# A hand-scheduled attention kernel: new waits and costs in its planner, longer joins on GpSimd, doubled sums

## The chip, the core and the metric

The kernel runs on one core of a Trainium2 chip. Its engines are TensorE (PE, matrix products; PEld in the profile is its weight loads), ScalarE (ACT, exponentials), VectorE (DVE), GpSimd (POOL) and SyncE (SP, which issues most DMAs). The metric is the device time of one execution in microseconds (us), median over runs.

## The reference

Two independent attention blocks of 32 heads with 16 columns each, on 2048 rows of 512, side by side in the output. Block A is linear attention, block B full softmax attention:

```python
# A
phi = lambda t: jnp.where(t > 0, t + 1, jnp.exp(t)) + 1e-6
pq, pk = phi(q), phi(k)
kv = jnp.einsum("bhsd,bhse->bhde", pk, v)
z = jnp.einsum("bhsd->bhd", pk)
o = jnp.einsum("bhqd,bhde->bhqe", pq, kv) / (jnp.einsum("bhqd,bhd->bhq", pq, z)[..., None] + 1e-6)
# B
scores = jnp.einsum("bhqd,bhkd->bhqk", q, k) * scale
o = jnp.einsum("bhqk,bhkd->bhqd", softmax(scores), v)
# both: q, k, v = x @ wqkv before, @ wo behind
```

B's scores are 32 x 2048 x 2048 numbers, and nearly all the time goes into their exponentials.

## The kernel before

**Blocks.** B's scores are made in blocks of 128 keys by 512 queries for one head. Four groups of eight heads, four stretches of 512 queries and two halves (even and odd heads) give 32 units; a unit has 4 heads (`g`, one in each quarter of TensorE's rows) times 16 blocks of keys, 64 blocks. A block's scores are one product QT,KM (L871, `qk`) into a bank of PSUM.

**Two ways to the exponential.** Either ScalarE applies Exp to two or three neighbouring banks of the tile pS at once and writes float16 to PT (L1084, in `fill_act_cand`). There are two such slots (`SCR`); a spare bank between them makes a slot three banks wide. Or VectorE does it without an exponential: it multiplies a block's scores (in pD or the spare bank) by a constant, adds another and stores int16 (L987, `p1`); the bits, read as float16, are a rough exponential. To smooth its error the block is used three times: the pattern itself, and two copies of it with a constant added to the bits, `SHIFT = (328, 656)`. Two blocks make a group of 1024 columns in one of eight buffers of DI (`DG`, `NDG`). The copies are made by GpSimd (L1176, `on_pool`) or, the second one alone and when GpSimd's queue is long, by VectorE (L1141, `on_dve`). GpSimd can make two copies of two groups in one instruction: two equal patterns, or the first of one group and the second of another, which it then makes out of that group's first (`mixed`).

**Sums.** The products with the values (L1253, `pv_cand`) add up numerator and denominator of four heads in one bank pPV: a block of PT takes one product with VV; a pattern takes one with VX (the values times `VW`, which weights the uncopied pattern, made by GpSimd in `v4_job`) and one with VV for each copy. A unit's sums go through VectorE (L1282, L1287, `unit_done`), GpSimd (L1288) and VectorE.

**The rest** are jobs in between: B's projections (L600, L677; K is spread to KM by DMAs on SP's queue), all of A (L718 to L783, with its own exponentials L693), and the output products (L809) and stores on SP's queue. PAR's column of SBUF is an operand of VectorE's L614, which makes the first K blocks.

**The order.** Every engine runs a fixed order of instructions, which a planner in the kernel's Python code writes when the program is built. It simulates the five lanes (`T`, with a clock for each), offers candidates (an exponential's two or three score products, `fill_act_cand`; more pattern blocks, `fill_d_cand`; products with the values, `pv_cand`; jobs, `job_cand`; what waits in `cands`), and takes the earliest, with priorities. It counts a duration for each instruction and a wait between engines: `LAT = 0.12` in most places, `LPE` behind a given engine. `SEG` is a table of 26 settings that change each 12 us of the planner's clock (limits on backlogs, how much earlier TensorE may run, when a second copy goes to VectorE, a seed for ties). `fill_in` puts products without a use into TensorE's gaps. On the chip semaphores keep the order safe, so a wrong duration costs waits and no correctness.

Of the kernel before, what the change touches and what calls it, by code (L numbers as in the profile page):

```python
# [238 lines left out]
def bass_concat_heads__linear_attn_block__softmax_full_mha__prompt_kernel(nc, A_x, A_wqkv, A_wo, B_x, B_wqkv, B_wo, out):  # L239
# [18 lines left out]
    VW = 1.5546875  # L258
    SHIFT = (328, 656)
    PMX = 0.0  # L260
# [64 lines left out]
    )  # L325
    GB = 0.0
    PM = -0.1
# [32 lines left out]
    with es:  # L360
# [51 lines left out]
        FLG = sb("FLG", [1, 1], F32)  # L412

# [75 lines left out]
        sch.add("dve", lambda e: e.memset(ZW[:], 0.0), writes=["ZW"])  # L489
        mk_ident(identb, "identb")  # L490
# [34 lines left out]
        LAT = 0.12  # L525
        LPE = {"dve": 0.04, "act": 0.19, "pool": 0.0, "pe": 0.12, "dma": 0.12}
# [6 lines left out]
        class Shared(float):  # L533

            pass

# [8 lines left out]
        class Job:  # L545
# [11 lines left out]
            def stage_done(self, i, end, bk, bi):  # L557
                if i == self.rel and bi is not None:
                    dfree[bi] = end + LPE[self.stages[i][0]]
                    held[bi] = False  # L560
                for st, tk in self.gives:
                    if st == i:
                        tok[tk] = end + LAT
                if i + 1 < len(self.stages):
                    eng, dur, fn = self.stages[i + 1]
                    lat = LAT if eng != "pe" or eng != self.stages[i][0] else 0.0
                    push(eng, end + lat, self.prio if eng == "pe" else (0 if eng == "act" or i + 1 <= self.rel and self.bank else min(self.prio, 2)), dur,
                         lambda st_, en_, fn=fn: (fn(bk), self.stage_done(i + 1, en_, bk, bi)))
# [10 lines left out]
        MM = 0.26  # L579
# [50 lines left out]
        def gram_x(t4, **kw):  # L630
# [6 lines left out]
            return Job(halves(mm, [("xTb", t) for t in ts], n=16, parts=2, dur=0.07) +  # L637
# [3 lines left out]
        def gram_w(kind, **kw):  # L641
# [5 lines left out]
            return Job(halves(mm, [("Wb", kind, g) for g in range(NGP)], n=16, parts=2, dur=0.07) +  # L647
# [8 lines left out]
        def flag_job(**kw):  # L656
            def f(e, bk):
# [6 lines left out]
                ("pe", 0.5, f_pe(f, [("TOP", i) for i in range(3)] + ["identf"])),  # L664
# [7 lines left out]
        def v4_job(t4, Gp, **kw):  # L672
# [7 lines left out]
            st = halves(mm, [("Wb", 2)] + [("xTb", t) for t in ts], n=16, parts=2, dur=0.07)  # L680
# [3 lines left out]
            st.append(("pool", 0.7, f_op("pool", lambda e: e.tensor_scalar(  # L684
# [29 lines left out]
        def akv_mm(t2, hp, kind):  # L714
# [5 lines left out]
            return chunked(halves(mm, ["WaK", ("xA", b)], n=8, parts=2, dur=0.14), 4 * hp + t2 // 4)  # L720
# [19 lines left out]
        def akvsum_job(hp, bl, **kw):  # L740
# [3 lines left out]
            st = halves(mm, [("KNa", t) for t in range(NT)] + [("VNa", t) for t in range(NT)] + ["VNa1"], n=16, parts=4, dur=0.085)  # L744
# [17 lines left out]
        def aden_job(sc, **kw):  # L762
# [6 lines left out]
            return Job(halves(mm, [("PQT", 0, bq) for bq in range(4)] + [("RHA", bq) for bq in range(4)] + [("RHZ", bq) for bq in range(4)], n=16, parts=2, dur=0.04) +  # L769
# [4 lines left out]
        def anum_job(sc, tl, **kw):  # L774
# [7 lines left out]
            return Job([("pe", 0.36, f_pe(f, [("PQT", 0, bq) for bq in range(4)] + [("RHA", bq) for bq in range(4)])),  # L782
# [143 lines left out]
        def d_pick(at, used, bi=None):  # L926
# [11 lines left out]
            if not dgroup["open"]:  # L938
                buf = min((i for i in range(NDG) if dgfree[i] is not None), key=lambda i: dgfree[i], default=None)
# [29 lines left out]
        def d_emit(tk, en):  # L969
# [4 lines left out]
            for b, buf, bi in tk:  # L974
# [23 lines left out]
                waiting[bi] = (buf, b, push("dve", en + LAT, 0, 0.6, p1))  # L998
# [17 lines left out]
        def fill_act_cand():  # L1016
# [16 lines left out]
            start = max(T["pe"], t0, afree[sl] + LAT, pw[0] - 0.5)  # L1033
            dur = 0.33 if pmode[0] != "q" else 0.23
            if nfill[0] >= 2 and not (u == NU - 1 and left[u] < DEND) and not lagging(start):
                lim = T["act"] + sum(exps) - dur - LAT - RW
# [4 lines left out]
            def run(st, en):  # L1041
# [25 lines left out]
                if len(bl) + len(tk) > 4:  # L1067
                    en += 0.21
# [418 lines left out]
        def fill_in(st):  # L1487
# [4 lines left out]
            if n <= 0:  # L1492
                return
# [188 lines left out]
```

## Time and profile before

| | |
|---|---|
| median of 2 runs | 661.1 us (661.04 to 661.15) |
| the profiled execution | 660.98 us, of which the profile's span is 659.2 us |
| TensorE's granted clock over the span | 0.999 |
| instructions | PE 6609, DVE 1089, ACT 686, POOL 450 |

A row of the groups reads: line, engine, operation, out<-in with shapes, count, then busy us, mean ns of one, and behind the last bar the engine's idle time before them with what ended it. A row of the timeline or of the chain begins with the start in us and the duration; xN merges N instructions. A row of the windows has the busy us of PE, PEld, DVE, ACT and POOL in this order, and in parentheses the instructions. A row of the waits has the us in total, the times and the longest. Records of neighbouring instructions overlap on an engine, so what one costs in a full queue is the spacing of starts, not the record's length.

### The profile page before, as it was taken

The numbers are of one execution on the slowest core, as the hardware profiler recorded it, in microseconds if no ns is written. First come the engines' busy times: TensorE is split into PE (matmuls) and PEld (weight loads), VectorE is DVE, ScalarE is ACT, GpSimd is POOL, SyncE is SP. The second block draws the span as 40 slices with busy tenths as digits, with TensorE's granted clock in tenths as the row PEclk, the third lists the DMA queues.
The fourth block names the chain that finished last, engine by engine and source line by source line (L and its number), as shares of the span: only waits on it lengthen the run. The fifth ranks groups of instructions, "written<-read, shape, count | busy, mean of one in ns | idle before, by whom it ended". The sixth has DMA issues, their size and how long they took to land.

```text
span 659.2 us, 15950 instructions
## 1 busy us (share of the span) xinstructions
PE 633.3 (96%) x6609; PEld 200.4 (30%) x6662; DVE 632.1 (96%) x1089; ACT 644.7 (98%) x686; POOL 592.7 (90%) x450
## 2 busy tenths in 40 slices
PE   8999999999999999999999999999999999999997
PEld 6323333222333333332222233322222223232222
DVE  4999999999999999999999999999999999999995
ACT  6999999999999999999999999999999999999994
POOL 5999999999999999999998899999999999999983
PEclk9999999999999999999999999999999999999999
DMA  9701010020102101210012011010011000120102
GB/s 178 207 3 33 1 34 6 11 43 9 34 2 33 21 14 33 65 34 9 9 27 64 17 34 34 18 19 10 7 26 41 17 1 11 25 26 25 33 26 67
DMA packets 53213, 21.53 MB, mean 33 GB/s; under 512 B 44177, under 2 KB 52625, under 8 KB 53137
## 3 DMA queue, kind: packets, MB, share of 16 engines
q1 hardware_dynamic: 51664, 19.80, 13.9%
q8 instruction: 54, 0.88, 0.6%
q10 hardware_dynamic: 1472, 0.66, 0.4%
q14 instruction: 23, 0.18, 0.1%
HBM read 4.46 MB, written 4.19 MB: 13 GB/s over the span
## 4 chain that ended last, share of the span: by engine, by line
ACT 96%; PE 3%; DMA 1%; ACTq 0%; issue 0%; DVE 0%; DVEq 0%
ACT PT L1084 93%; ACT EA L693 2%; DMA Wb<-in_B_wqkv_dram 1%; PE pPV L1253 1%; PE pD L809 1%; PE pS L871 0%; PE pD L1305 0%; PE pS L1305 0%; PE pS L1389 0%; ACTq L442 0%; PE pD L1389 0%; DVE KNa L582 0%; PE pD L659 0%; PE pD L871 0%; DVEq L1626 0%
## 5 line engine op out<-in xcount | busy, mean ns | idle before, releaser
L1084 ACT ACTIVATE PT<-pS 128x1024 f16<-128x1024 f32 (+1 forms) x648 | 636.6, 1305 | 1.0 <-PE pS L871 1.0
L1176 POOL TENSOR_SCALAR DI<-DI 128x2048 int16<-128x2048 int16 (+1 forms) x369 | 554.4, 1503 | 47.3 <-DVE DI L987 20.2
L987 DVE TENSOR_SCALAR DI<-pD 128x512 int16<-128x512 f32 x492 | 324.4, 679 | 6.1 <-PE pD L871 2.5
L871 PE MATMUL pS<-QT,KM 32*128 32x512 bf16 x1556 | 255.0, 384 | 8.8 <-ACT PT L1084 4.5
L1253 PE MATMUL pPV<-PT,VV 128*17 128x512 f16 x1369 | 233.7, 381 | 0.0
L1253 PE MATMUL pPV<-DI,VV 128*17 128x512 f16 x1358 | 227.3, 382 | 0.0
L871 PE MATMUL pD<-QT,KM 32*128 32x512 bf16 x492 | 170.5, 384 | 0.3 <-DVE PQT L696 0.3
L1253 PE MATMUL pPV<-DI,VX 128*17 128x512 f16 x679 | 161.0, 381 | 0.2 <-DVE OT L1282 0.2
L871 PEld LDWEIGHTS pS<-QT,KM 32*128 32x128 bf16 x1556 | 64.6, 91 | 265.3 <-ACT PT L1084 227.4
L987 DVE TENSOR_SCALAR DI<-pS 128x512 int16<-128x512 f32 x187 | 126.6, 677 | 0.7
L1141 DVE TENSOR_SCALAR DI<-DI 128x1056 int16<-128x1056 int16 x113 | 77.0, 687 | 0.5
L1253 PEld LDWEIGHTS pPV<-PT,VV 128*17 128x17 bf16 x1369 | 47.5, 88 | 41.4 <-issue 36.1
L1253 PEld LDWEIGHTS pPV<-DI,VV 128*17 128x17 bf16 x1358 | 47.0, 88 | 40.4 <-issue 33.0
L871 PEld LDWEIGHTS pD<-QT,KM 32*128 32x128 bf16 x492 | 40.5, 91 | 5.4 <-DVE DI L987 2.0
L1253 PEld LDWEIGHTS pPV<-DI,VX 128*17 128x17 bf16 x679 | 34.2, 88 | 22.0 <-issue 17.7
L718 PE MATMUL pD<-Wa,xTa 128*128 128x256 bf16 x200 | 30.5, 275 | 0.3 <-DVE DI L987 0.2
L600 PE MATMUL pD<-xTb,Wb 128*128 128x512 bf16 x67 | 21.2, 383 | 3.1 <-issue 2.3
L1282 DVE STREAM_TRANSPOSE OT<-pPV 128x512 f32<-128x512 f32 x31 | 21.9, 705 | 0.1
L582 DVE CAST KNa<-pD 128x512 bf16<-128x512 f32 x27 | 18.4, 681 | 3.0 <-PE pD L809 2.0
L1288 POOL TENSOR_TENSOR OT<-OT,ZR 128x256 bf16<-128x256 f32 x31 | 19.3, 621 | 1.6
L718 PEld LDWEIGHTS pD<-Wa,xTa 128*128 128x128 bf16 x200 | 15.4, 97 | 13.3 <-issue 6.3
L693 ACT ACTIVATE EA<-pD 128x512 bf16<-128x512 f32 x23 | 19.2, 835 | 0.0
(136 smaller groups left out, 346.3 us busy)
## 6 DMA issues: line engine op xcount, KB each, us to landing
out_dram<-KNa SPq DMA_DIRECT2D x31, 128.0 KB, 1.7
Wa<-in_A_wqkv_dram SPq DMA_DIRECT2D x1, 1536.0 KB, 8.2
KM<-KR SPq DMA_DIRECT2D x96, 16.0 KB, 1.8
Wb<-in_B_wqkv_dram SPq DMA_DIRECT2D x2, 384.0 KB, 4.5
Wb<-in_B_wqkv_dram SPq DMA_DIRECT2D x1, 512.0 KB, 4.6
Wa<-in_A_wo_dram SPq DMA_DIRECT2D x1, 512.0 KB, 4.5
Wa<-in_B_wo_dram SPq DMA_DIRECT2D x1, 512.0 KB, 3.7
ON<-in_B_x_dram ACTq DMA_DIRECT2D x1, 256.0 KB, 3.1
```

The source lines that it names most:

```text
L582: return lambda e, bk: (e.tensor_copy(out_fn(), in_fn(bk)) if lane == "dve" else e.activation(out_fn(), in_fn(bk), ACTF.Copy))
L600: return e.matmul(f32v(bk), lhsT=Wb[:, cc, kind * 512 + Gp * 128:kind * 512 + Gp * 128 + 128], rhs=xTb[:, cc, sc * 512:(sc + 1) * 512], st ...
L693: ("act", 0.052 + n * 0.000833, f_ev("act", lambda e, bk: e.activation(EA[:, 0:n], f32v(bk)[:, c0:c0 + n], ACTF.Exp), [], ["EA"])),
L718: return e.matmul(f32v(bk)[:, 256 * tt:256 * tt + 256], lhsT=xTa[:, b, cc, (o + tt) * 128:(o + tt + 1) * 128], rhs=Wa[:, cc, 512 * kind + ...
L871: return e.matmul(dst, lhsT=KM[32 * g:32 * g + 32, Gp % 2, e_, j * 128:(j + 1) * 128], rhs=QT[32 * g:32 * g + 32, Gp % 2, c * 512:(c + 1) ...
L987: sch.add("dve", lambda e: e.tensor_scalar(DI[:, di_at(0, buf) + i * 512:di_at(0, buf) + (i + n) * 512], f32v(DBANK[b0], n * 512), ESC, EB ...
L1084: sch.add("act", lambda e: e.activation(PTf[:, p0 * 512:p0 * 512 + w], S5[:, c0:c0 + w], ACTF.Exp, scale=SC), reads=skeys(sl, len(bl)), wr ...
L1141: sch.add("dve", lambda e: e.tensor_scalar(gapped(DI, di_at(v, buf), wide // 32, 32), DI[:, di_at(0, buf) - 32:di_at(0, buf) + w], 1.0, fl ...
L1176: sch.add("pool", lambda e: e.tensor_scalar(dv, sv, 1.0, sh_, op0=ALU.mult, op1=ALU.add), reads=keys, writes=[("DI", v_, x) for x, v_ in s ...
L1253: sch.add("pe", lambda e, g=g, j=j, c0=c0, V_=V_, r2=r2, P=P, first=first, last_=last_: e.matmul(PVb[32 * g:32 * g + 17, 0:512] if len(P.s ...
L1282: sch.add("dve", lambda e: e.transpose(OT[:, 0, :], PVb[:, 0:512]), reads=[("PV", g) for g in range(4)], writes=[("OT", 0)])
L1288: ("pool", 0.7, f_op("pool", lambda e: e.tensor_tensor(xn[:, :, 16 * e_:16 * e_ + 16], o[:, :, 0:16], zr.unsqueeze(2).broadcast_to([128, 1 ...
```

## The change

1. **The planner's waits.** `LAT` goes. A wait is looked up by the pair of engines (`LTO`) or by the engine that ends (`LPE`), and a change of kind among TensorE's products (scores, values, jobs) costs `SWT` in `pe_at`. Durations of jobs become shorter (a product of 512 columns 0.216 instead of 0.26). A score slot counts as free 0.426 after its exponential ends, where it was 0.07 + 0.12.
2. **The choice.** A product may come ahead of an exponential's scores only if it ends before `lim + KSL`. Products without a use go only into gaps of `FIDLE` = 0.8 or more. Pattern buffers are taken in turn.
3. **GpSimd's joins.** Up to `JN` = 4 copies of the same pattern from buffers at equal steps go into one instruction; the mixed pairs go. The planner counts `PFX` = 0.157 an instruction, where it counted 0.276.
4. **Doubled sums.** The constants that the copies add grow by 1024, which doubles the float16 value, `VW` doubles, and ScalarE's exponential gets a bias of ln 2 out of a column of SBUF, so that all terms of a sum double and the quotient stays.
5. **The table** `SEG` is new from end to end, so that the order on all engines changes.

```diff
-    VW = 1.5546875
-    SHIFT = (328, 656)
-    PMX = 0.0
+    VW = 2 * 1.5546875
+    SHIFT = (1352, 1680)
...
-    PM = -0.1
+    PM = 0.09
+    JN = 4
+    KSL = 0.02
+    PFX = 0.157
+    FIDLE = 0.8
...
+        LN2 = sb("LN2", [128, 1], F32)
+        sch.add("dve", lambda e: e.memset(LN2[:], 0.6931471805599453), writes=["LN2"])
...
-        LAT = 0.12
-        LPE = {"dve": 0.04, "act": 0.19, "pool": 0.0, "pe": 0.12, "dma": 0.12}
+        LPE = {"dve": 0.136, "act": 0.426, "pool": PM, "pe": 0.2, "dma": 0.12}
+        LTO = {("pe", "dve"): 0.2, ("pe", "act"): 0.215, ("act", "dve"): 0.4, ("dve", "pool"): 0.163, ("pool", "dve"): 0.07, ("dve", "act"): 0.15}
+        SWT = 0.106
+        def pe_at(md):
+            return T["pe"] + (0.0 if pmode[0] in (md, None) else SWT)
...
-                buf = min((i for i in range(NDG) if dgfree[i] is not None), key=lambda i: dgfree[i], default=None)
+                buf = min((i for i in range(NDG) if dgfree[i] is not None), key=lambda i: (dgfree[i] > at, (i - dgroup["buf"] - 1) % NDG), default=None)
...
-            start = max(T["pe"], t0, afree[sl] + LAT, pw[0] - 0.5)
-            dur = 0.33 if pmode[0] != "q" else 0.23
+            start = max(pe_at("q"), t0, afree[sl], pw[0] - 0.43)
+            dur = 0.214
...
-                    sch.add("act", lambda e: e.activation(PTf[:, p0 * 512:p0 * 512 + w], S5[:, c0:c0 + w], ACTF.Exp, scale=SC),
-                            reads=skeys(sl, len(bl)), writes=[("PT", p0 + i) for i in range(len(bl))])
-                    afree[sl] = en_ + 0.07
+                    sch.add("act", lambda e: e.activation(PTf[:, p0 * 512:p0 * 512 + w], S5[:, c0:c0 + w], ACTF.Exp, bias=LN2[:, 0:1], scale=SC),
+                            reads=skeys(sl, len(bl)) + ["LN2"], writes=[("PT", p0 + i) for i in range(len(bl))])
+                    afree[sl] = en_ + LPE["act"]
...
                 def on_pool(st_, en_):
-                    d1 = lambda b_: dgroup["st"][b_].get("v1", 1e9)
-                    two = [x for x in pshift if x[2] == w and x[1] != buf and x[3][0] <= st_ + PMW
-                           and (x[0] == v or d1(x[1] if v == 1 else buf) <= st_ + PMX)]
...
-                        T["pool"] = en_ = st_ + 0.276 + 2 * w * 0.00083
-                    mixed = len({v_ for _, v_ in segs}) == 2
+                    near_ = {x[1]: x for x in pshift if x[0] == v and x[2] == w and x[3][0] <= st_ + PMW}
+                    best = [buf]
+                    for step in range(1, NDG):
+                        run_ = [buf]
+                        while len(run_) < JN and run_[-1] + step in near_:
+                            run_.append(run_[-1] + step)
+                        while len(run_) < JN and run_[0] - step in near_:
+                            run_.insert(0, run_[0] - step)
+                        if len(run_) > len(best):
+                            best = run_
...
+                    T["pool"] = en_ = st_ + PFX + len(best) * w * 0.000834
+                    moves = [(di_at(0, b_), di_at(v, b_)) for b_ in best]
...
-                        return bass.AP(one.tensor, one.offset, [list(one.ap[0]), [offs[1] - offs[0], 2], [1, w]])
+                        return bass.AP(one.tensor, one.offset, [list(one.ap[0]), [offs[1] - offs[0], len(offs)], [1, w]])
...
-                    me = [(v, buf, w, push("pool", t_ + LAT + 0.05, 0, 0.276 + w * 0.00083, on_pool), rk)]
+                    me = [(v, buf, w, push("pool", t_ + LTO["dve", "pool"], 0, PFX + w * 0.000834, on_pool), rk)]
...
-            if n <= 0:
+            if n <= 0 or st - T["pe"] < FIDLE:
                 return
...
-                lim = max(dry - fa[1] - LAT - 0.05, fa[0])
-                keep = [o for o in opts if o[2] != "pe" or o[4] is fa[2] or o[0] + o[3] <= lim or o[0] + 1e-9 < fa[0] - o[3]]
+                lim = max(dry - 0.43, fa[0])
+                swt = lambda o: 0.0 if fd is not None and o[4] is fd[2] else SWT
+                keep = [o for o in opts if o[2] != "pe" or o[4] is fa[2] or o[0] + o[3] + swt(o) <= lim + KSL]
```

More of the change, by code (lines that the diff above doesn't have):

```diff
@@ L646, in gram_w @@
             gw = GRW[:, kind, :].rearrange("p (a h) -> p a h", h=8)
-            return Job(halves(mm, [("Wb", kind, g) for g in range(NGP)], n=16, parts=2, dur=0.07) +
+            return Job(halves(mm, [("Wb", kind, g) for g in range(NGP)], n=16, parts=2, dur=0.0555) +
                        [("dve", 0.6, f_ev("dve", lambda e, bk: e.tensor_reduce(GRW[:, kind, :], f32v(bk).rearrange("p (h c) -> p h c", c=16), axis=AX.X,
@@ L663, in flag_job @@
                                                 reads=[("GRX", i) for i in range(4)], writes=[("TOP", 0)])),
-                ("pe", 0.5, f_pe(f, [("TOP", i) for i in range(3)] + ["identf"])),
+                ("pe", 0.4, f_pe(f, [("TOP", i) for i in range(3)] + ["identf"])),
                 ("dve", 0.45, f_ev("dve", lambda e, bk: e.tensor_reduce(TP1[:, 0:3], bk[0][0:1, bk[2]:bk[2] + 384].rearrange("p (a n) -> p a n", n=128),
@@ L781, in f @@
                 return ins
-            return Job([("pe", 0.36, f_pe(f, [("PQT", 0, bq) for bq in range(4)] + [("RHA", bq) for bq in range(4)])),
+            return Job([("pe", 0.22, f_pe(f, [("PQT", 0, bq) for bq in range(4)] + [("RHA", bq) for bq in range(4)])),
                         ("dve", 0.6, f_ev("dve", lambda e, bk: e.tensor_tensor(
@@ L997, in p1 @@
                     chain(buf)
-                waiting[bi] = (buf, b, push("dve", en + LAT, 0, 0.6, p1))
+                waiting[bi] = (buf, b, push("dve", en + 0.2, 0, 0.598, p1))
         dgroup["st"] = {}
@@ L1066, in run @@
                     tk.append(d_take(pk))
-                if len(bl) + len(tk) > 4:
-                    en += 0.21
+                en = st + 0.214 * max(sum(x[2] == g for x in bl + [y[0] for y in tk]) for g in range(4))
+                T["pe"] = en
+                en = st + 0.214 * max(sum(x[2] == g for x in bl) for g in range(4))
                 c0 = 0 if sl == 0 else 1024 if ax else 1536
@@ L1110, in run @@
                     tk.append(d_take(pk2))
+                    if tk[0][0][2] == tk[1][0][2]:
+                        T["pe"] = en = en + 0.214
                 d_emit(tk, en)
-            return at, 0.32 if pmode[0] != "q" else 0.22, run
+            return at, 0.214, run
         def close_group():
@@ L1166, in on_pool @@
-                    mixed = len({v_ for _, v_ in segs}) == 2
-                    moves = sorted((di_at(1 if mixed and v_ == 2 else 0, b_), di_at(v_, b_)) for b_, v_ in segs)
+                    near_ = {x[1]: x for x in pshift if x[0] == v and x[2] == w and x[3][0] <= st_ + PMW}
[8 more added lines that the diff above has]
+                            best = run_
@@ new lines, in on_pool @@
+                    keys = []
+                    for b_ in best:
+                        x = near_.get(b_, me[0])
+                        pshift.remove(x)
+                        if b_ != buf:
+                            cands["pool"].remove(x[3])
+                            st_ = max(st_, x[3][0])
+                        keys += [("DI", 0, b_, i) for i in range(n)]
+                    T["pool"] = en_ = st_ + PFX + len(best) * w * 0.000834
+                    moves = [(di_at(0, b_), di_at(v, b_)) for b_ in best]
@@ L1242, in pv_cand @@
             bt = bb[2]
[L1243 removed]
+            dur = 0.218 * bb[1]
             def run(st, en):
@@ L1359, in fin @@
                                               reads=kst(tl), queue="act" if tl == 2 else "sp", force_signal=True))
-                    urgent2.append(Job([("pe", 0.22, last), (lane, 0.6 if lane == "dve" else 0.52, fin)], [("onh", h), ("tail", tl)], [], bank=False))
+                    urgent2.append(Job([("pe", 0.216, last), (lane, 0.6 if lane == "dve" else 0.52, fin)], [("onh", h), ("tail", tl)], [], bank=False))
         def warm(n):
@@ L1462, in job_cand @@
             best = None
-            bi = min((i for i in range(NB + JX) if dfree[i] is not None), key=lambda i: (max(dfree[i], T["pe"]), i), default=None)
+            bi = min((i for i in range(NB + JX) if dfree[i] is not None), key=lambda i: (max(dfree[i], pe_at("j")), i), default=None)
             for lst, pr in ((urgent, 0.5), (early, 2), (bjobs, 2.2), (urgent2, 2.3), (ajobs, AJP)):
@@ L1502, in fill_in @@
                 dst, wr, acc = DB[0:17, db[0] * 512:db[0] * 512 + 256], ("D", db[0]), None
-            elif any(a_ is not None and a_ + LAT <= T["pe"] and i != tail["so"] for i, a_ in enumerate(afree)):
-                sl = min(i for i in range(2) if afree[i] is not None and afree[i] + LAT <= T["pe"] and i != tail["so"])
+            elif any(a_ is not None and a_ <= T["pe"] and i != tail["so"] for i, a_ in enumerate(afree)):
+                sl = min(i for i in range(2) if afree[i] is not None and afree[i] <= T["pe"] and i != tail["so"])
                 g, first = 0, True
```

85 lines of the change are left out of this document (31 added, 54 removed), and 102 rows, old and new, of the table SEG.

## The prediction

> **What bounds the kernel now.** I read the page first, for the busy shares and the chain that ended last.
>
> ```profile
> span 659.2 us, 15950 instructions
> PE 633.3 (96%) x6609; PEld 200.4 (30%) x6662; DVE 632.1 (96%) x1089; ACT 644.7 (98%) x686; POOL 592.7 (90%) x450
> ...
> ACT 96%; PE 3%; DMA 1%; ACTq 0%; issue 0%; DVE 0%; DVEq 0%
> ```
>
> Four engines are 90% busy or more, but the chain is ScalarE's for 96% of the span. The view by windows, asked for the steady part from 60 to 600 us, says how hard:
>
> ```profile
> 60.00:600.00 540.00, 523.26 (x5525) 162.22 (x5565) 531.45 (x911) 540.00 (x580) 499.55 (x354) 1.00 0.12 24
> ```
>
> The fourth busy number is ScalarE's: 540.00 of 540.00. The timeline and the chain of waits give its two ends:
>
> ```profile
> 8.73 37.01 ACT PT L1084 x37
> ...
> 291.69 9.17 ACT PT L1084 x10
> ```
> ```profile
> 629.01 20.77 ACT L1084 ACTIVATE PT<-pS 128x1024 f16<-128x1024 f32 x18
> ```
>
> The exponentials run from 8.73 us to 629.01 + 20.77 = 649.8 us; ahead stand 8.7 us of loads and first projections, behind 9.4 us of last products and stores. The span of 659.2 plus 1.8 outside it is the profiled execution's own 660.98 us, 0.1 below the median of 661.1. So the time moves only if the stretch of 641 us does: by fewer blocks for ScalarE, or by another price for each. The price is 9.17 / 10 = 0.917 us from one exponential of two blocks to the next, or 0.46 us a block.
>
> The groups by shape say how the 2048 blocks (4 groups of heads, 8 units, 64 blocks each) are divided:
>
> ```profile
> L1084 ACT ACTIVATE PT<-pS 128x1024 f16<-128x1024 f32 x575 | 560.5, 1260 | 0.0
> L1084 ACT ACTIVATE PT<-pS 128x1536 f16<-128x1536 f32 x73 | 121.5, 1664 | 1.0 <-PE pS L871 1.0
> ```
> ```profile
> L987 DVE TENSOR_SCALAR DI<-pD 128x512 int16<-128x512 f32 x492 | 324.4, 679 | 6.1 <-PE pD L871 2.5 <-PE pS L871 1.2
> L987 DVE TENSOR_SCALAR DI<-pS 128x512 int16<-128x512 f32 x187 | 126.6, 677 | 0.7
> L1141 DVE TENSOR_SCALAR DI<-DI 128x1056 int16<-128x1056 int16 x113 | 77.0, 687 | 0.5
> ```
> ```profile
> L1176 POOL TENSOR_SCALAR DI<-DI 128x2048 int16<-128x2048 int16 x198 | 376.3, 1900 | 28.1 <-DVE DI L987 13.9 <-POOL DI L1176 2.0 <-DVE RD L770 0.2
> L1176 POOL TENSOR_SCALAR DI<-DI 128x1024 int16<-128x1024 int16 x169 | 176.9, 1047 | 18.2 <-DVE DI L987 6.3
> ```
>
> ScalarE takes 575 x 2 + 73 x 3 = 1369 blocks in 648 instructions. VectorE turns 492 + 187 = 679 into int16 patterns. Each pair of these (a group) needs two shifted copies of 1024 elements; 113 copies are VectorE's and about 198 x 2 + 169 = 565 GpSimd's, in 367 instructions (1.54 copies each). A block leaves ScalarE only if VectorE and GpSimd have time for it.
>
> **The change, part by part.**
>
> *Joins of up to four.* Two doubles that follow each other, and two singles:
>
> ```profile
> 249.99 3.88 POOL L1176 TENSOR_SCALAR DI<-DI 128x2048 int16<-128x2048 int16 x2 [0.40 <-DVE DI L987]
> ...
> 301.27 2.17 POOL L1176 TENSOR_SCALAR DI<-DI 128x1024 int16<-128x1024 int16 x2
> ```
>
> From start to start a double takes 3.88 - 1.90 = 1.98 us and a single 2.17 - 1.05 = 1.12. A copy's elements cost 1.90 - 1.05 = 0.85, so 0.27 is the price of an instruction. Joins save only that. The new rule joins only equal patterns in evenly spaced buffers, so the old pairs of first and second pattern are lost; and a queue that often runs dry cannot offer four copies:
>
> ```profile
> POOL DI L1176 <- DVE DI L987: 15.9, 42, 1.0
> POOL DI L1176 <- POOL DI L1176: 1.9, 12, 0.2
> ```
>
> (GpSimd's waits from 60 to 600 us.) The ends are no gain in joins, 1.54, and four everywhere, 565 / 4 = 141 instructions. I take 2.2, 257 instructions, between the row of doubles, which is nearest, and what a longer queue adds. It saves (367 - 257) x 0.27 = 30 us of GpSimd.
>
> What is that worth? Move x blocks off ScalarE and y copies from VectorE back to GpSimd; all three must fall by the same 0.46x. VectorE's prices stand in its timeline:
>
> ```profile
> 17.50 0.68 DVE L987 TENSOR_SCALAR DI<-pS 128x512 int16<-128x512 f32 x1
> 18.10 0.68 DVE L987 TENSOR_SCALAR DI<-pD 128x512 int16<-128x512 f32 x1
> 18.70 0.74 DVE L614 TENSOR_SCALAR KM<-pD,PAR 128x512 bf16<-128x512 f32 x1
> 19.35 0.69 DVE L1141 TENSOR_SCALAR DI<-DI 128x1056 int16<-128x1056 int16 x1
> 19.96 0.74 DVE L614 TENSOR_SCALAR KM<-pD,PAR 128x512 bf16<-128x512 f32 x1
> 20.62 0.68 DVE L681 CAST VV<-pD 128x512 bf16<-128x512 f32 x1
> ```
>
> An eviction is 18.10 - 17.50 = 0.60, a shifted copy 19.96 - 19.35 = 0.61. VectorE: 0.60x - 0.61y = -0.46x, so y = 1.74x. GpSimd: (0.85 + 0.27 / 2.2)(x + y) - 30 = -0.46x, or 3.12x = 30, x = 9.6. ScalarE falls by 9.6 x 0.46 = 4.4 us. The ends are 0 without joins and, with 61 us saved at a copy price of 0.92, x = 20.5 and 9.4 us.
>
> *Exponentials with a bias.* Sums double: the copies go up by 1024 more (an octave of the bit pattern), VW doubles, and all 640-odd exponentials take `bias=LN2[:, 0:1]`, a column in SBUF, where no bias was given. No row shows ScalarE with such an operand. VectorE's nearest does: with PAR's column an eviction of that size takes 19.35 - 18.70 = 0.65 and 20.62 - 19.96 = 0.66 against 0.60, so 0.06 us more. The ends are 0 and 0.06 an instruction; a fetch can only add, which excludes a gain. I take 0, because the engines overlap differently: VectorE's records exceed their spacing by 0.68 - 0.60 = 0.08, and by 0.74 - 0.655 = 0.08 with the column, so nothing hid there; ScalarE's exceed it by 1.26 - 0.917 = 0.34, so an exponential is under way 0.34 us before its predecessor is done, more than a fetch of 0.06. ScalarE is the chain, so if that cover fails it all shows: 643 x 0.06 = 39 us.
> The Trainium skill (ScalarE: Activation LUTs, What ACT_TABLE_LOAD costs) speaks against this part: it gives 186 ns plus 0.833 ns an element with immediate operands, about 93 ns more for each pointer operand, and an overlap of 93 ns between neighbours. No run here shows that price; by it the sum would be an estimated 643 x 0.093 = 60 us longer, 716 us.
>
> *LN2's memset* is one small VectorE instruction before the first exponential, where VectorE waits anyway; its wait on ScalarE is met before 8.73 us. Nothing:
>
> ```profile
> 0.00:8.70 8.70, 7.24 (x71) 6.38 (x71) 2.82 (x12) 2.47 (x4) 7.45 (x26) 1.00 0.83 164
> ```
>
> VectorE (third) is busy 2.82 of 8.70 us. Without that cover it costs about 0.1.
>
> *Waits in the planner, SWT, the rule with KSL.* These add no instruction; they move instructions in the five fixed orders. The old planner took a score buffer as free 0.07 + 0.12 = 0.19 us after an exponential; the waits say:
>
> ```profile
> PEld pS L871 <- ACT PT L1084: 227.4, 522, 0.7
> ```
>
> 227.4 / 522 = 0.44 a time, and behind that wait TensorE's weight products queue. The new 0.426 puts other products ahead of it. But ScalarE has no idle time between 60 and 600 us to recover, so the gain is 0. At worst a product put ahead overruns; the start of the next exponential is late next. From the other side, what better waits can free is VectorE's 540 - 531.45 = 8.5 us and GpSimd's 15.9 + 1.9: half of both is x = (8.9 + 1.6 x 4.3) / 3.12 = 5, or 2.3 us (1.6 is GpSimd's 0.97 a copy by VectorE's 0.61).
>
> *FIDLE* drops filler products in gaps under 0.8 us. There are 24, none of use to the result, and with TensorE 523 of 540 us busy the clock (the 1.00 in the row) has no reason to fall: nothing. *The new order and the round robin of buffers* move the K spreads and stores on SP's queue, each behind the same producer as before, and no transfer stands in the steady chain; the product of VX stays one GpSimd instruction a tile. Nothing on the sum, 1 us either way for the tail.
>
> **The sum.** Start 8.7 as before, exponentials 641.1 - 4.4 + 0, tail 9.4 as before, 1.8 outside the span: 656.6 us against 661.0, or 656.7 on the scale of the median. Its own range is 649 (four everywhere, and half the waits) to 661 (no gain).
>
> **The rivals.**
>
> *The column costs on ScalarE (slower).* For it: VectorE pays in full for PAR's. Against it: the 0.34 us of overlap. With VectorE's 0.06 it is 656.7 + 39 = 695 us; the engines differ, so I spread the price from half to one and a half of that, 0.03 to 0.09, which gives 676 to 715 us. It decides from 0.03 upward, since 643 x 0.028 = 18 us takes the time past 2%. The order stays fixed, so nothing moves to the engines that then idle. The page of the Trainium skill named above speaks for this case.
>
> *GpSimd is planned too cheap.* The new formula has 0.157 an instruction where the trace has 0.27. On 257 instructions the plan lacks 257 x 0.113 = 29 us. GpSimd's spare time in the steady part is 15.9 + 1.9 of 540, 21 us over the stretch. If the plan fills it as full as now, 8 us are left over; products wait for copies, TensorE's queue stands, and exponentials start late: 656.7 + 8 = 665 us, still within 2%. For it: every such pair in the timeline shows 0.27. Against it: VectorE and not GpSimd may be filled first. It decides once 21 us are used up.
>
> *More than the sum.* Four everywhere and all the waits recovered: 661.1 - 9.4 - 4.6 = 647 us. Against it is the dry queue.
>
> *The change doesn't do what it says:* joins stay at 1.54, 661 us; this is the end of my range.
>
> **How the numbers follow.** The sum's case, 649 to 661, has 0.37; GpSimd too cheap, 661 to 673, 0.21; the column, 676 to 715, 0.34, which is high because the one row with a column shows its price in full; more than the sum, 0.08. A measurement of this kernel can tell about 2% from no change, 648 to 674. So faster is 0.08, same 0.37 + 0.21 = 0.58, slower 0.34. The range must reach into the column's case: 648 to 704 leaves out 0.08 below and, with prices spread evenly, 11 / 39 of 0.34 = 0.10 above.
>
> **What would show it.** Joins: fewer L1176 rows, with shapes of 3072 or 4096 elements, about 257 in all, and fewer shifted copies of VectorE. Blocks: about 1359 instead of 1369 products of PT. Column: the spacing of exponentials in the chain, 0.917 (free) or 0.98 to 1.01. GpSimd too cheap: TensorE or ScalarE waiting on GpSimd, and idle time in ScalarE's 60 to 600 us. The prediction is wrong if that spacing grows by more than 0.03 us, or if ScalarE falls under 99% there.

## The result and the profile after

The changed kernel takes 731.58 us (median of 2 runs, 730.18 and 732.98) against 661.1: 1.107 times as long, 95% interval 1.098 to 1.116. I had forecast 656.7 in a range of 648 to 704. The measured time lies outside it: 70 us were lost where 4 were to be won.

The page of the profile after (the profiled execution took 732.98 us), first the busy shares, then the chain that ended last:

```profile
span 731.2 us, 15899 instructions
...
PE 655.8 (90%) x6646; PEld 202.2 (28%) x6646; DVE 636.1 (87%) x1074; ACT 699.5 (96%) x682; POOL 615.0 (84%) x457
...
ACT 93%; PE 3%; DMA 1%; SPq 1%; DVE 0%; issue 0%; DVEq 0%
```

The span grew by 72.0 us and ScalarE's busy time by 54.8, with four instructions fewer on it. ScalarE is still the chain. Two pieces of the exponentials in the chain of waits, ten of them in a row and a long piece near the end:

```profile
271.15 10.04 ACT PT L1099 x10
...
657.81 57.33 ACT PT L1099 x49
```

Ten take 10.04 us, where the ten at 291.69 took 9.17 before: 0.087 us more each. (Over all of them, the commonest spacing of starts goes from 0.904 to 0.995 us for two blocks and from 1.331 to 1.422 for three, 0.091 more in both.) The view by windows, the steady part:

```profile
60.00:600.00 540.00, 488.45 (x5016) 147.69 (x5013) 487.65 (x818) 527.35 (x520) 471.05 (x319) 1.00 0.09 20
```

ScalarE, the fourth number, has 12.65 us without work where it had none, though each instruction of it takes longer. The timeline of ScalarE shows where most of that is, in two stretches without work (holes, below), and TensorE's beside it shows what stood in front (the number in brackets is the idle time before the row, and what ended it):

```profile
512.48 13.48 ACT L1099 ACTIVATE PT<-pS,LN 128x1024 f16<-128x1024 f32 x13
535.43 11.16 ACT L1099 ACTIVATE PT<-pS,LN 128x1024 f16<-128x1024 f32 x11 [9.47 <-PE pD L887]
549.37 2.12 ACT L1099 ACTIVATE PT<-pS,LN 128x1024 f16<-128x1024 f32 x2 [2.78 <-PE pD L887]
```
```profile
528.67 1.89 PE L616 MATMUL pD<-xTb,Wb 128*128 128x512 bf16 x8
530.40 1.03 PE L616 MATMUL pS<-xTb,Wb 128*128 128x512 bf16 x4
531.26 1.03 PE L616 MATMUL pD<-xTb,Wb 128*128 128x512 bf16 x4
533.55 0.38 PE L887 MATMUL pD<-QT,KM 32*128 32x512 bf16 x1 [1.26 <-DVE KR L635]
```

From 525 us on the last group's projections of K and Q come in a burst, and from 524.4 to 533.5 us no score product runs. The chain of waits shows what they wait for. K is cast into one of two buffers of KR and spread from there to KM by eight DMAs, so the third cast can't start before the first one's spread has landed, and until then its projection holds the bank pD that a score product needs. SyncE's queue, the chain and VectorE:

```profile
526.55 4.96 SPq L640 DMA_DIRECT2D KM<-KR  x8
```
```profile
530.93 1.79 DMA KM<-KR
```
```profile
532.80 0.69 DVE L635 CAST KR<-pD 128x512 bf16<-128x512 f32 x1 [2.26 <-DMA KM<-KR]
```

In the kernel before the last four casts of K start within 44 us, from 442 to 486; here within 8, from 526 to 534.

The groups by shape:

```profile
L1099 ACT ACTIVATE PT<-pS,LN 128x1024 f16<-128x1024 f32 x567 | 612.7, 1440 | 12.6 <-PE pD L887 12.3 <-PE pS L887 0.4
L1191 POOL TENSOR_SCALAR DI<-DI 128x2048 int16<-128x2048 int16 x182 | 345.3, 1897 | 27.4 <-DVE DI L1003 15.6
...
L1191 POOL TENSOR_SCALAR DI<-DI 128x1024 int16<-128x1024 int16 x173 | 180.7, 1044 | 35.9 <-DVE DI L1003 23.8
...
L1099 ACT ACTIVATE PT<-pS,LN 128x1536 f16<-128x1536 f32 x77 | 143.1, 1859 | 1.0 <-PE pS L887 1.0
```

ScalarE has 567 x 2 + 77 x 3 = 1365 blocks (1369 before). GpSimd has 173 single copies, 182 doubles, 16 triples and one of four: 589 copies in 372 instructions, 1.58 each where there were 1.54 (four small ones of 512 are left out). The joins of up to four hardly came about.

For a tally I call ScalarE's lost time what passes between the start of its first exponential and the end of the last beyond the usual spacings (0.904 or 0.995 us for two blocks, 1.331 or 1.422 for three, 0.477 for A's exponentials): 19.6 us, where it was 8.8. Of the 19.6, 12.6 are idle time. So 644 x 0.091 = 58.6 us is the exponentials' price, 10.8 the lost time, 4.2 the tail (13.6 us from the last exponential on, 9.4 before), 0.3 the start, and -1.8 the four blocks: 72.1 for 72.0. That is a tally and no cause yet, since the order of all engines changed with the price.

### The profile page after: what moved, and what is told of

Same layout as the page of the kernel before. It is cut to its first block, busy times and chain, and to the rows that moved or that the text cites. A ratio compares the mean times of both kernels' runs of the same rounds, so it can differ in the third digit from the quotient of the medians.

```text
span 731.2 us, 15899 instructions
## 1 busy us (share of the span) xinstructions
PE 655.8 (90%) x6646; PEld 202.2 (28%) x6646; DVE 636.1 (87%) x1074; ACT 699.5 (96%) x682; POOL 615.0 (84%) x457
## 4 chain that ended last, share of the span: by engine, by line
ACT 93%; PE 3%; DMA 1%; SPq 1%; DVE 0%; issue 0%; DVEq 0%
ACT PT L1099 91%; ACT EA L709 2%; PE pPV L1266 1%; DMA xTb<-in_B_x_dram 1%; PE pS L887 1%; PE pD L825 1%; SPq L640 1%; DMA KM<-KR 0%; DMA out_dram<-KNa 0%; PE pS L825 0%; PE pS L1402 0%; DVE KR L635 0%; DVE KNa L598 0%; PE pS L1318 0%; PE pD L616 0%
## 5 line engine op out<-in xcount | busy, mean ns | idle before, releaser
L1099 ACT ACTIVATE PT<-pS,LN 128x1024 f16<-128x1024 f32 (+1 forms) x644 | 694.1, 1490 | 13.7 <-PE pD L887 12.3
L1191 POOL TENSOR_SCALAR DI<-DI 128x1024 int16<-128x1024 int16 (+2 forms) x376 | 576.1, 1532 | 83.4 <-DVE DI L1003 58.5
L1003 DVE TENSOR_SCALAR DI<-pD 128x512 int16<-128x512 f32 x492 | 328.9, 682 | 39.1 <-PE pD L887 22.7
L1266 PE MATMUL pPV<-DI,VV 128*17 128x512 f16 x1366 | 232.3, 383 | 0.0
L1266 PE MATMUL pPV<-DI,VX 128*17 128x512 f16 x683 | 155.0, 383 | 0.1
L1003 DVE TENSOR_SCALAR DI<-pS 128x512 int16<-128x512 f32 x191 | 130.1, 681 | 6.5 <-PE pS L887 4.6
L1158 DVE TENSOR_SCALAR DI<-DI 128x1056 int16<-128x1056 int16 x89 | 60.3, 685 | 0.2
L734 PE MATMUL pD<-Wa,xTa 128*128 128x256 bf16 x200 | 29.8, 275 | 0.0
L616 PE MATMUL pD<-xTb,Wb 128*128 128x512 bf16 x96 | 26.6, 382 | 0.0
L709 ACT ACTIVATE EA<-pD 128x512 bf16<-128x512 f32 x26 | 24.3, 934 | 0.0
L1301 POOL TENSOR_TENSOR OT<-OT,ZR 128x256 bf16<-128x256 f32 x31 | 19.2, 620 | 4.0 <-DVE ZR L1300 1.9
```

Of the source, the lines that this page charges most:

```text
L616: return e.matmul(f32v(bk), lhsT=Wb[:, cc, kind * 512 + Gp * 128:kind * 512 + Gp * 128 + 128], rhs=xTb[:, cc, sc * 512:(sc + 1) * 512], st ...
L709: ("act", 0.052 + n * 0.000833, f_ev("act", lambda e, bk: e.activation(EA[:, 0:n], f32v(bk)[:, c0:c0 + n], ACTF.Exp), [], ["EA"])),
L734: return e.matmul(f32v(bk)[:, 256 * tt:256 * tt + 256], lhsT=xTa[:, b, cc, (o + tt) * 128:(o + tt + 1) * 128], rhs=Wa[:, cc, 512 * kind + ...
L1003: sch.add("dve", lambda e: e.tensor_scalar(DI[:, di_at(0, buf) + i * 512:di_at(0, buf) + (i + n) * 512], f32v(DBANK[b0], n * 512), ESC, EB ...
L1099: sch.add("act", lambda e: e.activation(PTf[:, p0 * 512:p0 * 512 + w], S5[:, c0:c0 + w], ACTF.Exp, bias=LN2[:, 0:1], scale=SC), reads=skey ...
L1158: sch.add("dve", lambda e: e.tensor_scalar(gapped(DI, di_at(v, buf), wide // 32, 32), DI[:, di_at(0, buf) - 32:di_at(0, buf) + w], 1.0, fl ...
```

## The experiments

All times are medians beside runs of the kernel before on the same chip (660.94 to 661.18 us). An "order" is the order in which the planner writes the instructions. Where an edit shows a piece of a line, the rest of the line stays.

| kernel | us | ratio to before, 95% |
|---|---|---|
| column alone, order before (e2) | 717.85 | 1.084 to 1.088 |
| after without the column (e1) | 701.75 | 1.060 to 1.064 |
| after without column and doubling (e3) | 698.28 | 1.054 to 1.058 |
| e3 with only the constants doubled (e7) | 701.9 | 1.059 to 1.064 |
| e3, GpSimd at 0.273 (e4) | 684.21 | 1.033 to 1.037 |
| e3, table searched anew (e12) | 687.07 | 1.038 to 1.041 |
| e4, table searched anew (e10) | 666.48 | 1.007 to 1.010 |
| e10 with column and doubling (e13) | 723.31 | 1.092 to 1.096 |
| after, GpSimd at 0.273 (e11) | 741.73 | 1.120 to 1.124 |
| before, GpSimd at 0.157 (e6) | 696.75 | 1.052 to 1.056 |
| before, GpSimd at 0.290 (e9) | 687.58 | 1.039 to 1.043 |
| e4 without SWT (e5) | 702.56 | 1.059 to 1.064 |
| e3 without SWT (e8) | 700.84 | 1.058 to 1.062 |

### The column

**e1: ln 2 as an immediate.** The values stay doubled.

```diff
-ACTF.Exp, bias=LN2[:, 0:1], scale=SC)
+ACTF.Exp, bias=0.6931471805599453, scale=SC)
```

> The changed kernel with the bias of ln 2 as an immediate number of the instruction and no column; nothing else moves, the order of every engine is the same. Theory A (the column costs on every exponential, 644 x 0.091 us = 59 us, and the rest of the 70 us is the order's: 10 us more waiting of ScalarE in the stretch and 4.5 us more tail): the spacing of doubles falls from 0.995 back to 0.904 us, time 673 us. Theory B (column alone, the order's holes come from ScalarE being slower than planned and go with it): 657 to 661 us. Theory C (the new order as a whole costs, an immediate other than zero costs as much as a column): stays near 730 us.

Measured: 701.75 us, between the theories; none was whole. The chain of waits has the old price again (8.26 / 9 = 0.918), and the view by windows shows ScalarE with 28.7 us of idle time:

```profile
492.38 8.26 ACT PT L1099 x9
```
```profile
60.00:600.00 540.00, 508.77 (x5212) 162.69 (x5234) 496.97 (x853) 511.30 (x542) 492.06 (x335) 1.00 0.10 21
```

The waits from 60 to 600 us name what is new in it:

```profile
PEld pPV L1266 <- POOL DI L1191: 27.2, 54, 1.4
...
PE pPV L1266 <- POOL DI L1191: 8.7, 19, 0.9
```

In the same instructions with the column, the first of these waits was this:

```profile
PEld pPV L1266 <- POOL DI L1191: 2.2, 9, 0.3
```

So the column had slowed ScalarE until GpSimd was no longer late. ScalarE's lost time is 19.6 us with the column and 48.4 without: 28.8 us appear as 58.6 go, and of the medians 731.58 - 701.75 = 29.8 us are left as the column's cost in this order.

**e2: a column of zeros in the kernel before** (the column ZC and its memset are added). Order and values are those of before.

```diff
-ACTF.Exp, scale=SC)
+ACTF.Exp, bias=ZC[:, 0:1], scale=SC)
```

> The kernel before with one thing added: its exponentials read their bias of 0 out of a column of zeros in SBUF. Order, copies and sums are those of before. Theory A: 648 x 0.091 us = 59 us more, 720 us. If a column cost what it costs VectorE, 0.06: 700 us. If the column cost only in the new order: 661 us.

Measured: 717.85 us, 56.9 more. ScalarE is busy for all of the 540 us again, and does less in them (534 instructions for 580):

```profile
60.00:600.00 540.00, 491.14 (x5065) 146.49 (x5096) 499.17 (x838) 540.00 (x534) 457.68 (x329) 1.00 0.11 22
```

In an order that keeps ScalarE full, every exponential pays: 56.9 / 648 = 0.088 us, measured on the whole.

### The price of a GpSimd instruction in the planner

**e3: no doubling either.** e1 with the old constants, the old VW and no bias: the change's planner, joins and table alone.

```diff
-    VW = 2 * 1.5546875
-    SHIFT = (1352, 1680)
+    VW = 1.5546875
+    SHIFT = (328, 656)
```

> The changed kernel with the sums as before: copies by +328 and +656, the single weight, no bias; its planner, joins, table and order stay. All theories: the same as with the immediate bias within 1 us, since only data differ. If the doubled values themselves mattered to an engine, the two differ.

Measured: 698.28 us. The new order alone costs 37 us, and TensorE's waits on GpSimd stay (24.4 us of weight loads from 60 to 600).

**e4: the traced price.** e3 with one number:

```diff
-    PFX = 0.157
+    PFX = 0.273
```

> As the run without doubling, but the planner counts 0.273 us an instruction for GpSimd's copies, as the trace has it, in place of 0.157. The order changes with it and its table was not made for it, so a few us either way are the order's luck. If GpSimd planned too cheap cost time (rival of the prediction), TensorE's waits on GpSimd go and the time falls below that run's; if GpSimd is not what is waited for, it is the same or slower, 673 to 685 us.

Measured: 684.21 us, 14.1 less. The waits on GpSimd are gone (0.7 us of weight loads), and ScalarE's idle time from 60 to 600 us falls from 27.9 to 10.7. The loss that is left, 23 us, is something else: 8.8 us of it are a longer tail (18.2 us).

**e6: the mirror.** The kernel before, planned with the low price:

```diff
-0.276 + 2 * w * 0.00083
+0.157 + 2 * w * 0.00083
...
-0.276 + w * 0.00083
+0.157 + w * 0.00083
```

> The kernel before, its planner counting 0.157 in place of 0.276 us an instruction for GpSimd's copies; its old pairs, sums and table stay, the order follows. If too cheap a GpSimd costs by itself (its price theory): 670 to 690 us, with TensorE waiting on GpSimd, where before had no such wait. If the price is harmless in itself: 661 to 668 us, the luck of an order that its table was not made for.

Measured: 696.75 us, 35.6 more, with the same wait:

```profile
PEld pPV L1253 <- POOL DI L1176: 29.1, 57, 1.7
```

But any new number also gives an order that the table of settings was not searched for. So there had to be a control.

**e9: the control.** The same edit, with 0.290 in place of 0.157.

> The kernel before with its planner's price for a GpSimd copy 5% too dear instead of far too cheap (0.276 us to 0.290 in the two formulas); same instructions, only the order is planned anew with a table that was searched for 0.276. This is the control for the 35.6 us that 0.157 cost in the same planner. Theory F (the too cheap price itself is what cost): a price that is off by 0.014 us sends no more work to GpSimd than it can do, no wait of TensorE on its copies comes back, and only the unfitted table shows: 665 to 675 us. Theory G (any order that the table was not searched for costs that much): 690 us or more, and 0.157 has shown nothing about the price.

Measured: 687.58 us, 26.6 more: between the theories, nearer to G. No wait on GpSimd comes (2.3 us); the loss is 11.0 us of tail, where exponentials ended at 639.55 + 24.90 = 664.45 us and 20.4 more passed (9.4 before), 9.9 us of ScalarE's lost time, about half of it in the hole shown, and 5 us of 12 blocks more (563 x 2 + 85 x 3 = 1381):

```profile
317.79 20.35 ACT L1084 ACTIVATE PT<-pS 128x1024 f16<-128x1024 f32 x21
341.03 0.60 ACT L693 ACTIVATE EA<-pD 128x512 bf16<-128x512 f32 x1 [2.90 <-PE pD L755]
343.94 1.02 ACT L1084 ACTIVATE PT<-pS 128x1024 f16<-128x1024 f32 x1 [2.31 <-PE pS L871]
```
```profile
639.55 24.90 ACT L1084 ACTIVATE PT<-pS 128x1536 f16<-128x1536 f32 x22
671.18 0.60 ACT L582 ACTIVATE KNa<-pS 128x512 bf16<-128x512 f32 x1 [6.73 <-PE pS L1305]
```

By the times alone, only some 9 of e6's 35.6 us are left for the price, and e3 against e4 could have been luck of the order too. The traces part the two further: e6 has 43.4 us of lost time and a tail of 12.0, e9 has 18.7 and 20.5. So the control's loss sits in another place for the most part, and the wait on GpSimd stands only in e6.

### The table

For the next two the 26 settings in each 12 us were searched anew, with the end of the planner's own simulation as the aim; no other line is changed.

**e10: the traced price and a table for it** (e4 with a new `SEG`, e.g. its first row):

```diff
-        (0.0,0.3,4,3.0,4,2,6,2,9.5,36,2.5,7.0,0.5,0.8,2,5.0,1.5,2.5,1.0,2,1,0.3,10,20,0,0),
+        (0.0,0.3,4,3.0,6,1,8,2,9.5,30,2.5,7.0,0.8,2.5,2,4.0,2.0,2.5,0.5,2,1,0.3,4,0,0,0),
```

> The changed kernel without bias column and doubling, GpSimd's instruction priced at the traced 0.273 us (684.21 us so far), and its table of 12 us rows searched anew for that price, so that the planner sees ScalarE idle for a quarter as long. Theory H (what was left of the loss, 23 us above the kernel before, was an order with a table that does not fit): the holes of 10 and 9 us in ScalarE go, 665 to 674 us, so the new waits are about as good as the old ones and no better. Theory I (the new waits themselves plan worse orders): it stays at 680 to 690. If the new waits are truer than the old ones, as the change means them, 655 to 661.

Measured: 666.48 us, 17.7 less than e4. ScalarE is full (539.57 of 540):

```profile
60.00:600.00 540.00, 520.58 (x5465) 163.55 (x5503) 523.46 (x899) 539.57 (x578) 495.12 (x396) 1.00 0.10 23
```
```profile
L1100 ACT ACTIVATE PT<-pS 128x1024 f16<-128x1024 f32 x576 | 563.9, 1296 | 1.2 <-PE pS L888 0.8 <-PE pD L888 0.4
...
L1192 POOL TENSOR_SCALAR DI<-DI 128x1024 int16<-128x1024 int16 x280 | 293.2, 1047 | 29.6 <-DVE DI L1004 9.9
...
L1100 ACT ACTIVATE PT<-pS 128x1536 f16<-128x1536 f32 x76 | 127.6, 1679 | 1.0 <-PE pS L888 1.0
```

Theory H stands. It is 5.5 us above the kernel before, which is about the 11 blocks more that ScalarE has (576 x 2 + 76 x 3 = 1380; 11 x 0.46 = 5). It comes without more joins: 280 copies are single. So the new waits, with the right price and a table that fits, plan about as well as the old ones and no better.

**e12: the low price and a table for it.** e3 with a new `SEG`.

> The changed kernel without bias column and doubling, GpSimd's instruction still priced 0.157 us, and the table of 12 us rows searched anew for that price, as it was for 0.273 (which gave 666.48 us). Theory L (the price is a fault of its own): GpSimd gets more than it can do, TensorE waits again on its copies for 15 us or more, 677 to 690 us. Rival M (only the fit of the table mattered): few such waits, 664 to 672 us.

Measured: 687.07 us, 20.6 above e10. The waits from 60 to 600 us:

```profile
PEld pPV L1267 <- POOL DI L1192: 20.6, 48, 1.1
...
PE pPV L1267 <- POOL DI L1192: 4.6, 10, 0.8
```

Theory L stands: this search did not repair the low price, whose waits the planner does not see. The two searches were not of the same length and gave two different tables, so 20.6 is good to a few us at best. ScalarE's lost time says the same three times over: 32.0 us in e12 and 10.2 in e10, 46.6 in e3 and 20.3 in e4, 43.4 in e6 and 18.7 in e9, so the low price goes with 22 to 26 us more of it in each pair.

**e13: e10 with the whole doubling.** Same order, with column, constants and VW of the change.

> The order of the 666.48 us kernel (price 0.273, table searched anew) with the whole of the doubling put back: the bias column, +1352 and +1680, doubled VW. The order is the same instruction by instruction. Theory N (a column costs 0.091 us an exponential wherever ScalarE has no idle time): 652 x 0.091 = 59 us more, 724 to 727 us, a little less where ScalarE's end of the program was idle before. Rival O (in the new order the column costs the 30 us that it cost in the changed kernel): 693 to 700 us.

Measured: 723.31 us, 56.8 more. The same 44 exponentials in the chain of waits, without and with the column:

```profile
123.83 43.41 ACT PT L1100 x44
```
```profile
136.14 47.28 ACT PT L1100 x44
```

(47.28 - 43.41) / 44 = 0.088 us. Theory N stands: the cost is whole again where ScalarE has no idle time.

**e11: the traced price in the changed kernel as it is.**

```diff
-    PFX = 0.157
+    PFX = 0.273
```

> The changed kernel with one number changed: GpSimd's instruction planned at 0.273 us instead of 0.157; bias column and doubled sums stay. Theory J (the column makes ScalarE so slow that it covers GpSimd's lateness): the 14 us that this number was worth without the column are hidden, and only ScalarE's holes and the exponentials' floor count: 724 to 735 us. Rival K (the costs of the column and of the price add up): 731.6 - 14 = 717 us or less.

Measured: 741.73 us, 10.2 more, which neither theory had. J's half holds: under the column the low price costs nothing that this takes away. But the order that came out is worse for two other reasons: its tail is 18.8 us for 13.6, and ScalarE has 12 blocks more (579 x 2 + 73 x 3 = 1377), 6.2 us. Its holes, 6.0 us at 535 and 1.6 behind it, are smaller than those of the changed kernel (9.5 and 2.8). With an unfitted table, 10 us either way is within what a new order does.

### What told less

**e7: only the constants of the copies** (e3 with `SHIFT = (1352, 1680)`; the patterns are then double and the rest is not, so it serves for its time alone).

> The run with sums not doubled (698.3 us), with the copies' constants alone at +1352 and +1680; weight and exponentials are single, so the terms of a sum no longer fit each other and the values are off. It asks what made the 3.5 us between the doubled run with an immediate and the run without doubling. If GpSimd's instructions take longer with the large constants (copy to normalisation 1.96 in place of 1.86 us): 701 to 702 us. If it was the weight or the bias: 698.

Measured: 701.9 us, 3.6 above e3, the whole step from e3 to e1. What differs in the trace is GpSimd's queue where the kind of instruction changes: the same place in GpSimd's timeline, e3 first.

```profile
84.67 0.62 POOL L1301 TENSOR_TENSOR OT<-OT,ZR 128x256 bf16<-128x256 f32 x1
85.26 13.50 POOL L1191 TENSOR_SCALAR DI<-DI 128x2048 int16<-128x2048 int16 x6
```
```profile
85.33 0.62 POOL L1301 TENSOR_TENSOR OT<-OT,ZR 128x256 bf16<-128x256 f32 x1
86.01 13.49 POOL L1191 TENSOR_SCALAR DI<-DI 128x2048 int16<-128x2048 int16 x6
```

From the product L1301 to the next copy it is 0.59 us with 328 and 656, and 0.68 with 1352 and 1680; doubles behind each other are equally far apart in both (1.98 us). That this makes the 3.6 us is argued from the late GpSimd of this order, not shown.

**e5 and e8: no charge for a change of kind on TensorE** (`SWT = 0.0` in e4 and in e3).

> The run with GpSimd priced at 0.273 (sums not doubled, no bias), and in the planner SWT = 0 in place of 0.106: no charge for a change of kind among TensorE's products. Table and joins stay. Theory D (the charge keeps jobs from being let ahead of an exponential's scores, they pile up, K of the last quarter comes in a burst near 490 us and the pattern blocks pause near 310 us): the casts of K spread out again, the 10 us pause of evictions and ScalarE's 8 us hole go, time 662 to 670 us. Rival E (the switch is a true cost of TensorE, and without the charge its queue runs late everywhere): ScalarE waits on TensorE in small pieces, 685 us or more.

> The fourth corner: SWT = 0, but GpSimd counted at 0.157 an instruction as in the change (sums not doubled, no bias). If the two constants cost separately, this stands above the corner with 0.273 by about the 14 us that the price made before: 676 to 684 us, with TensorE waiting on GpSimd's copies. If the price only mattered together with the starved jobs, it is the same as that corner within 4 us.

Measured: 702.56 us (18.4 above e4) and 700.84 (2.6 above e3). Theory D fell: from 60 to 600 us the large holes do go in e5, but many small waits take their place, as rival E has it (the weight loads of TensorE's score products wait 64.6 us of the whole span on nothing but their own issue, in 192 places). Between these two the low price costs nothing: e8, which has it, is 1.7 us the faster. Its waits are there (15.0 us of weight loads on GpSimd for 3.2), and ScalarE's lost time is 56.8 us for 50.8, but ScalarE has 20 blocks fewer (1352 for 1372). So what the price costs depends on the rest of the planner too. Since each has a table that was not searched for it, and e9 shows what that alone does, these two don't settle what the charge is worth.

## Why the prediction was wrong

Both signs of being wrong that the prediction named came: the spacing grew by 0.091 us (the limit was 0.03), and ScalarE is busy for 527.35 of 540 us, 97.7% (the limit was 99%).

**The step that failed** is the bias column: "I take 0, because the engines overlap differently". It costs 0.091 us an exponential, 57 us in a full order and 30 in the changed kernel's. The 0.34 us of overlap was misread. It came from the mean record of 1.26 us. The row of e9 above at 343.94, an exponential with idle time ahead of it, lasts 1.02; the 0.24 us more in a full queue I take for waiting on the predecessor. So the true overlap is 1.02 - 0.904 = 0.11 us. With the column the like row, e11's, is

```profile
471.26 1.11 ACT L1099 ACTIVATE PT<-pS,LN 128x1024 f16<-128x1024 f32 x1 [0.39 <-PE pD L887]
```

and 1.11 - 0.995 = 0.115: the overlap is the same and the record is longer by the whole price, so nothing covers it. VectorE's 0.06, the upper end that I had, was too low as well. The rule of the Trainium skill (ScalarE: Activation LUTs, What ACT_TABLE_LOAD costs), about 93 ns for a pointer operand, agrees with the measured 0.091. I gave the column's case, 676 to 715 us, 0.34 and cut my range inside it. The measured time lies above that whole case as well, since the other terms failed too.

**"GpSimd is planned too cheap"** had the right mechanism, named by its wait (TensorE on copies), and the wrong size; in the changed kernel itself the column hides it (2.2 us of such waits). I let the plan overrun by 8 us, after the spare time was used up. Without the column, measured is 14.1 us (e3 to e4) and 20.6 with tables searched for both (e10 to e12), and nothing without the charge SWT (e5 to e8). Two terms of it fell: I took 257 instructions where there are 372, 372 x 0.113 = 42 us lacking; and copies came late in many places, each with TensorE's queue behind it, before the mean was full (in e3 GpSimd is busy for 492.25 of 540 us, and TensorE's weight loads wait on it 50 times).

**Joins at 2.2** failed: 1.58. The prediction saw both reasons, the old mixed pairs lost and a queue that often runs dry, and still took a gain of 4.4 us; the four blocks fewer are worth 1.8. That the fitted e10 has 1.34 copies an instruction (557 in 417) and is 32 us faster than e3 shows that joins were not what limited the order.

**The waits in the planner ("the gain is 0") and the new order ("Nothing on the sum, 1 us either way for the tail")** failed too. A table that doesn't fit its planner costs 18 us (e4 to e10) to 27 us (e9), in holes where projections bunch, in the tail and in blocks. My argument was that ScalarE had no idle time to win; that was right for a gain and did not bound the loss. And "no transfer stands in the steady chain" did not hold for the new order: K's spread stands in the chain just ahead of the largest hole in the changed kernel, e1, e3 and e7 and across it in e4, e9 and e11. From 60 to 640 us it stands nowhere in the chain of the orders whose table was searched for them (before, e10, e12). That is read from the traces; no run gives KR a third buffer or spaces out the projections, so what the holes would be worth by that is open. Which of the new waits, or the rule with `KSL`, makes an order better or worse, no run separates either.

LN2's memset and FIDLE at nothing had no run of their own. The clock stayed at 1.00 in the steady part, as expected.

**How the 70 us divide.** By one path of runs: planner, waits and joins with a right price and a fitted table +5.5 (e10); the low price +20.6 (e12); the table as the change has it +11.2 (e3); constants +3.6 (e7); doubled VW about 0 (e1); the column +29.8 (after). By another: the column and doubling +56.8 on top of e10, and then price and table +8.3 (e13 to after). Both sum to 70. The shares depend on the path, because a slower ScalarE hides a late GpSimd and the other way round. The price in each path goes with the orders that it made, and a new order alone moves the time by 10 us or more (e9, e11). Open is how much of +11.2 is the table and how much luck of one order. No version here beats the kernel before; the nearest, e10, is 0.7 to 1.0% above it.

## What to carry to other kernels

Take an engine's overlap from a record that waited for nothing, or from the spacing of starts, never from the mean record of a full queue; and give a constant bias as an immediate, since a column costs each instruction on the engine that is the chain. In a kernel with a planner, a changed price is two changes, the price and an order that its settings were not searched for, so run a control with a harmless change of the same number, and search the settings again on both sides before comparing. Before calling an order's loss luck, follow the chain of waits through its largest hole. Two bottlenecks of like size hide each other: undo each alone and both before adding their costs.

## What the runs showed of the hardware that I had not expected

An immediate bias costs ScalarE nothing (0.918 us for two blocks in e1's chain against 0.917 with no bias), the column 0.091, the same for two blocks and for three. Eight DMAs of 16 KB in a row on SyncE's queue take 4.96 us to issue, and the last has landed 1.79 us after its own issue began. On GpSimd, larger constants in a copy can cost about 0.1 us at a neighbour of another kind (0.59 to 0.68 us) and cost nothing between copies (1.98 us from double to double in both). Over all runs the small constants give 0.59 in many places (16 of 31 in e3) and 0.685 or more in the rest, the large ones never under 0.685; why stays open.
